# Window attention, forward and backward, on one core: y and z turned to token order by one DMA transpose per quad, the gradient turned on the PE array, and P and dS stacked into one stationary of 128 rows

## The chip, the core and the metric

One core of a Trainium2 chip runs the program. Its engines each work through their own list of instructions: PE (TensorE, the 128x128 matmul array; loads of its stationary operand are shown apart as PEld), DVE (VectorE), ACT (ScalarE), POOL (GpSimd) and SP (SyncE, which here only starts DMA transfers). Instructions of different engines wait for each other by semaphores. Matmuls write into PSUM, which has eight banks of 128 x 512 f32; DVE or ACT must move a result out (evict it) before its bank can be used again. The metric is the device time of one execution in microseconds; smaller is better.

## What is computed

Window attention over an image of 256 x 256 pixels with 384 channels in windows of 8 x 8 = 64 tokens, and its gradients with respect to x, wqkv and wo for a given grad_out:

```python
def _fwd_reference(x, wqkv, wo):
    ...
    xw = xw.reshape(B * nh * nw, win * win, C)
    qkv = xw @ wqkv
    q, k, v = (qkv[..., :C].copy(), qkv[..., C:2 * C].copy(), qkv[..., 2 * C:].copy())
    scale = C ** (-0.5)
    p = _softmax(jnp.einsum('bqc,bkc->bqk', q, k) * scale, axis=-1)
    o = jnp.einsum('bqk,bkc->bqc', p, v) @ wo
    ...
def reference(x, wqkv, wo, grad_out):
    _out, _vjp = jax.vjp(_f, x, wqkv, wo)
    _grads = _vjp(grad_out)
    return (_out0, *[jnp.asarray(_g) for _g in _grads])
```

All inputs and outputs are bf16. There are 1024 windows.

## The kernel before

The kernel never forms q, k and v. It folds the weights once at the start into four 384 x 384 matrices: A (query times key weights, scaled), its transpose AT, B (value times output weights) and its transpose BT. Per window, with x its tokens and g the incoming gradient, it computes y = x A and z = g BT (the program has them with channels on the partitions), the scores S = y x^T and the gradient of P, z x^T, in one PSUM tile `sd`, then P (softmax) and dS (`Sb`), u = x B, v = x AT, the output `po` = P u, and the gradient of x, `pd` = P^T z + dS^T y + dS v. For the weight gradients it forms `pu` = dS x and `pw` = P^T g per window and sums x^T times these over all windows into `GF_acc`.

Tiling: two windows, one above the other, make a tile of 128 tokens (`dram_tile`); the lower 64 partitions (`LO`) hold one window, the upper 64 (`HI`) the other. Four tiles make a quad; there are 128 quads. With 384 channels a row, `CK` = 3 blocks of 128 channels.

The main loop runs one `step` per quad, as a pipeline over three quads: c (the quad before), b (this quad) and a (the next). The order of every engine's instructions is the order in which `step` writes them (`manual_schedule`). In a step PE does, in this order: `scores` of b (24 matmuls); u and v (`uv`) of b's tiles 0 and 1; `attend` of c's tiles 0 and 1; a filler; `uv` of tiles 2 and 3; `yz_tok`, 24 PE transposes that turn y and z of b to token order; `attend` of c's tiles 2 and 3; `turn`, 16 small transposes of P and dS; `project` of a, 18 matmuls for z and y; a filler. A filler is one piece of `gf_group`: 12 matmuls that sum over three finished quads into one bank, and one addition into `GF_acc` by DVE. `soft` (on DVE and ACT) is written between these pieces.

`attend` works on 64 x 64 blocks. Its inner function `both` issues four matmuls with 64 rows and 64 columns each, two windows times two results, which occupy the four quarters of the array; a tile has three such groups, of which three halves go to `pd`: `Pb` with `zq`, `Sb` with `yq`, `ST` with `vq`. The four results of a tile take four PSUM banks: ACT evicts `po` (to `osb`) and `pd` (to `dsb`), DVE evicts `pu` and `pw`.

PSUM: the pool `ring` has seven banks that all pieces share in the order in which they come free, and `ps_sd` has one for the scores. Before its first matmul, a piece waits for the eviction that gives back the bank it is to use.

Transfers: `load` reads four tiles of x on SP's queue and four of grad_out on POOL's, two quads ahead, and then has SP issue two DMA transposes of 12 blocks of 128 x 128 each, `dT` from the gradient and `xT` from x. The stores of `osb` go out on SP's queue, those of `dsb` on POOL's, in two halves per tile. SP and POOL also work strictly in order.

The tables that say which engine evicts what, and the pace of the pipeline, stand ahead of the loop:

```python
EV = {"z": "AAA", "y": "DAD", "u": "AAAA", "v": "AAAA", "o": "AAAA", "U": "DDDD", "W": "DDDD", "d": "AAAA"}
AHEAD = 2
```

Of the kernel before, what the change touches and what calls it, by code (L numbers as in the profile page):

```python
# [9 lines left out]
ALU = mybir.AluOpType  # L10
# [12 lines left out]
def kernel(  # L23
# [83 lines left out]
    def dram_tile(ap, bp, t):  # L107
        return ap[0, 2 * WIN * bp:2 * WIN * (bp + 1), WIN * t:WIN * (t + 1), :]

    LO, HI = slice(0, WT), slice(WT, P)  # L110

    def load(st):
        bp, t0 = st["at"]
        st["xq"] = xq = grp.tile([P, QUAD, C], BF16, tag="xq", name="xq", bufs=2 * GQ + 3)
        st["dq"] = dq = qp.tile([P, QUAD, C], BF16, tag="dq", name="dq", bufs=5)
        for t in range(QUAD):
            nc.sync.dma_start(out=xq[:, t, :], in_=dram_tile(x, bp, t0 + t))
            nc.gpsimd.dma_start(out=dq[:, t, :], in_=dram_tile(grad_out, bp, t0 + t))  # L118
        st["xT"] = xT = qp.tile([P, QUAD, CK, P], BF16, tag="xT", name="xT", bufs=3)
        st["dT"] = dT = qp.tile([P, QUAD, CK, P], BF16, tag="dT", name="dT")  # L120
        for src, dst in ((dq, dT), (xq, xT)):
            nc.sync.dma_start_transpose(out=dst[:].rearrange("p t m k -> p (t m) k"),
                                        in_=src[:].rearrange("p t c -> p (t c)"))

    ENG = {"D": nc.vector.tensor_copy, "A": nc.scalar.copy}

    def project(st, kind, mo):
        if kind == 0 and mo == 0:
            st["yz"] = qp.tile([P, CK, QUAD, 4, WT], BF16, tag="yz", name="yz")
            st["zc"] = qp.tile([P, CK, QUAD, 2, WT], BF16, tag="zc", name="zc")  # L130
        yz = st["yz"]
        wgt, src = ((BT_sb, st["dT"]), (A_sb, st["xT"]))[kind]
        pj = ring.tile([P, QUAD, 2, WT], F32, tag="r")
        for m in range(CK):
            nc.tensor.matmul(pj[:].rearrange("p t w k -> p (t w k)"), lhsT=wgt[:, m, mo * P:(mo + 1) * P],  # L135
                             rhs=src[:, :, m, :], start=(m == 0), stop=(m == CK - 1))
        if kind == 0:
            ENG[EV["z"][mo]](out=yz[:, mo, :, 0:4:3, :], in_=pj[:])  # L138
            nc.vector.tensor_copy(out=st["zc"][:, mo, :, :, :], in_=yz[:, mo, :, 0:4:3, :])
        else:  # L140
            ENG[EV["y"][mo]](out=yz[:, mo, :, 1:3, :], in_=pj[:])  # L141

    def scores(st):
        yz, xT = st["yz"], st["xT"]
        st["sd"] = sd = ps_sd.tile([P, QUAD, 2, WT], F32, tag="sd", name="sd")
        for t in range(QUAD):
            for w in range(2):
                for m in range(CK):
                    nc.tensor.matmul(sd[:, t, w, :],  # L149
                                     lhsT=yz[:, m, t, 2 * w:2 * w + 2, :].rearrange("p s k -> p (s k)"),  # L150
                                     rhs=xT[:, t, m, w * WT:(w + 1) * WT],
                                     start=(m == 0), stop=(m == CK - 1))
# [4 lines left out]
    def soft(st, step):  # L157
# [14 lines left out]
        elif step == 3:  # L172
# [4 lines left out]
            nc.vector.reciprocal(out=ri[:], in_=rs[:])  # L177
            st["Pb"] = Pb = qp.tile([P, QUAD, WT], BF16, tag="Pb", name="Pb")
            nc.vector.tensor_tensor(out=Pb[:], in0=ex[:], in1=over_k(ri[:]), op=ALU.mult)
        elif step == 4:  # L180
            st["pr"] = pr = sm.tile([P, QUAD, WT], F32, tag="pr", name="pr")
            for w, h in ((0, LO), (1, HI)):
# [3 lines left out]
        else:  # L186
            pd = sm.tile([P, QUAD, WT], F32, tag="pd")
            nc.vector.tensor_tensor(out=pd[:], in0=st["Pb"][:], in1=over_k(st["D"][:]), op=ALU.mult)
            st["Sb"] = Sb = qp.tile([P, QUAD, WT], BF16, tag="Sb", name="Sb")
            nc.vector.tensor_tensor(out=Sb[:], in0=st["pr"][:], in1=pd[:], op=ALU.subtract)  # L190

    def uv(st, t, part):
        if t == 0 and part == 0:
            for n in ("uq", "vq", "yq", "zq"):
# [8 lines left out]
    def yz_tok(st, t, part):  # L203
        src, dst = ((st["yz"][:, :, t, 1:3, :], st["yq"]), (st["zc"][:, :, t, :, :], st["zq"]))[part]
        pt = ring.tile([P, CK, P], BF16, tag="r")
        for m in range(CK):
            nc.tensor.transpose(pt[:, m, :], src[:, m, :, :].rearrange("p w k -> p (w k)"), ident[:])  # L207
        nc.vector.tensor_copy(out=dst[:, t, :].rearrange("p (m c) -> p m c", m=CK), in_=pt[:])

    def turn(st, kind):  # L210
        src, n = ((st["Pb"], "PT"), (st["Sb"], "ST"))[kind]
        st[n] = dst = qp.tile([P, QUAD, WT], BF16, tag=n, name=n)
        pt = ring.tile([P, QUAD, WT], BF16, tag="r")
        for t in range(QUAD):
            for h in (LO, HI):
                nc.tensor.transpose(pt[h, t, :], src[h, t, :], ident[h, h])  # L216
        nc.vector.tensor_copy(out=dst[:], in_=pt[:])

    def attend(st, t):
        bp, t0 = st["at"]  # L220
        if t == 0:
            st["Uq"] = grp.tile([P, QUAD, C], BF16, tag="Uq", name="Uq")
            st["Wq"] = grp.tile([P, QUAD, C], BF16, tag="Wq", name="Wq")
        po = ring.tile([P, C], F32, tag="r", name="po")
        pd = ring.tile([P, C], F32, tag="r", name="pd")
        pu = ring.tile([P, C], F32, tag="r", name="pu")
        pw = ring.tile([P, C], F32, tag="r", name="pw")

        def both(straight, crossed):
            for h, o, (dst, lhs, rhs, first, last) in ((LO, LO, straight), (LO, HI, crossed), (HI, LO, crossed),  # L230
                                                       (HI, HI, straight)):
                nc.tensor.matmul(dst[o, :], lhsT=st[lhs][h, t, :], rhs=st[rhs][h, t, :], start=first, stop=last)  # L232

        both((po, "PT", "uq", True, True), (pd, "Pb", "zq", True, False))
        osb = ob.tile([P, C], BF16, tag="o")
        ENG[EV["o"][t]](out=osb[:], in_=po[:])  # L236
        nc.sync.dma_start(out=dram_tile(out_0, bp, t0 + t), in_=osb[:])
        both((pu, "ST", "xq", True, True), (pd, "Sb", "yq", False, False))
        ENG[EV["U"][t]](out=st["Uq"][:, t, :], in_=pu[:])  # L239
        both((pw, "Pb", "dq", True, True), (pd, "ST", "vq", False, True))  # L240
        dsb = ob.tile([P, C], BF16, tag="d")
        ENG[EV["d"][t]](out=dsb[:], in_=pd[:])  # L242
        for h, w in ((LO, 1), (HI, 0)):
            nc.gpsimd.dma_start(out=dram_tile(out_1, bp, t0 + t)[WIN * w:WIN * (w + 1)], in_=dsb[h, :])  # L244
        ENG[EV["W"][t]](out=st["Wq"][:, t, :], in_=pw[:])  # L245

    fill = []

# [17 lines left out]
            except StopIteration:  # L266
                fill.pop(0)

    def step(c, b, a):

        def on(st):
            return (lambda f, *r: f(st, *r)) if st is not None else (lambda f, *r: None)
        C_, B, A = on(c), on(b), on(a)
# [8 lines left out]
        C_(attend, 0)  # L282
        B(soft, 3)
        C_(attend, 1)
        B(soft, 4)
        filler(1)
        B(uv, 2, 0)
        B(uv, 2, 1)
        B(soft, 5)
        B(uv, 3, 0)  # L290
        B(uv, 3, 1)
        for t in range(QUAD):
            B(yz_tok, t, 0)
            B(yz_tok, t, 1)
        C_(attend, 2)
        C_(attend, 3)
        B(turn, 0)
        B(turn, 1)
        for kind in range(2):
            for mo in range(CK):  # L300
                A(project, kind, mo)
        filler(1)

    EV = {"z": "AAA", "y": "DAD", "u": "AAAA", "v": "AAAA", "o": "AAAA", "U": "DDDD", "W": "DDDD", "d": "AAAA"}
# [3 lines left out]
    AHEAD = 2  # L308
    with tc.manual_schedule(engines=MANUAL):
        for i in range(min(AHEAD, n)):  # L310
            load(sts[i])
        held = []
        get = lambda i: sts[i] if 0 <= i < n else None
        for i in range(-1, n + 1):
            if AHEAD <= i + AHEAD < n:
                load(sts[i + AHEAD])
            step(get(i - 1), get(i), get(i + 1))
            if i > 0:
                held.append(sts[i - 1])
                sts[i - 1] = None  # L320
# [64 lines left out]
```

## Time and profile before

| | |
|---|---|
| median of three runs | 2295.58 us (2294.31 to 2297.17) |
| the profiled execution | 2295.61 us, its span 2293.8 us |
| PE busy | 2231.7 us (97% of the span), clock 1.00 |
| DVE, ACT, POOL busy | 1827.0, 1259.5, 867.2 us |
| transposes of y and z on PE (L207), 128x128 | 3072, of 219 ns each with its pipeline |
| their copies out of PSUM by DVE (L208) | 1024, 346 and 345 ns |
| matmuls of `attend` (L232), 64x64 with 384 columns | 6144, 325 to 341 ns with their pipeline |
| DMA transposes on SP's queue | 256, of 12 blocks |
| bytes moved by DMA | 308.59 MB |

The profile is that of one execution. The chain of work that ended last is followed back from the last instruction: at each step to what released it. A matmul's duration in a table is longer than the time it holds the array, since matmuls are pipelined; the time that the array is held is the distance from one start to the next. Releasers, in square brackets, are inferred from semaphores. `pj`, `pt`, `pg`, `po`, `pd`, `pu` and `pw` are PSUM tiles: projections and u, v (`pj`), transposes (`pt`), fillers (`pg`) and the four results of `attend`.

### The profile page before, as it was taken

The page shows a single profiled execution, that of the slowest core. Times are in us where ns is not written, and L with a number is a line of the kernel's source. Part 1 is how long each engine was busy: PE and PEld are TensorE (multiplying, and loading weights), DVE is VectorE, ACT ScalarE, POOL GpSimd, SP SyncE. Part 2 cuts the span into 40 slices and gives each one's busy share as a digit, 9 for nine tenths or more (in the row PEclk, how much of TensorE's full clock was granted, in tenths as well). Part 3 has the DMA queues.
Part 4 walks back from the last instruction along what each step waited for, and adds up shares of the span by engine and source line. Part 5 has one row for each costly group of instructions (what it writes and reads, how often), then busy time and mean ns, then how long its engine had stood idle before and what let it go on. Part 6 is the DMA issues. An engine that isn't in the chain of part 4 may idle for free.

```text
span 2293.8 us, 59316 instructions
## 1 busy us (share of the span) xinstructions
PE 2231.7 (97%) x22910; PEld 1334.9 (58%) x22910; DVE 1827.0 (80%) x4771; ACT 1259.5 (55%) x2701; POOL 867.2 (38%) x1542
## 2 busy tenths in 40 slices
PE   7999999999999999999999999999999999999998
PEld 4555555555555555555555555555555555555555
DVE  6878887888788878877887788778878887888786
ACT  4555555555555555555555555555555555555553
POOL 3443333334333343343334333433333343334332
PEclk9999999999999999999999999999999999999999
DMA  7666555665565556555656565656556655655542
GB/s 165 143 142 135 137 131 135 138 139 133 138 139 132 133 138 138 133 135 135 142 131 142 134 141 128 143 134 138 129 135 139 139 132 139 138 133 134 137 114 60
DMA packets 624475, 308.59 MB, mean 135 GB/s; under 512 B 458816, under 2 KB 607040, under 8 KB 624192
## 3 DMA queue, kind: packets, MB, share of 16 engines
q1 hardware_dynamic: 550064, 203.49, 42.1%
q0 software_dynamic: 73728, 101.02, 15.6%
q8 instruction: 179, 2.93, 0.5%
q14 instruction: 104, 0.85, 0.1%
q10 hardware_dynamic: 400, 0.29, 0.0%
HBM read 101.84 MB, written 101.84 MB: 89 GB/s over the span
## 4 chain that ended last, share of the span: by engine, by line
PE 95%; ACT 3%; DVE 1%; issue 0%; DMA 0%; ACTq 0%
PE pg L256 22%; PE pj L135 22%; PE pj L199 21%; PE pt L207 7%; PE po L232 5%; PE pw L232 5%; PE sd L149 4%; PE pd L232 3%; PE pu L232 2%; PE pt L216 2%; ACT osb L236 2%; PE pc L97 0%; ACT uq L201 0%; DMA w_sb<-in_wqkv_dram 0%; ACT vq L201 0%
## 5 line engine op out<-in xcount | busy, mean ns | idle before, releaser
L244 POOL DMA_DIRECT2D out_dram<-dsb x1024 | 575.9, 570 | 1388.2 <-ACT dsb L242 1365.6
L201 ACT CAST uq<-pj 128x384 bf16<-128x384 f32 x512 | 245.3, 479 | 635.1 <-PE pj L199 632.9
L256 PEld LDWEIGHTS <-xq 128*128 128x128 bf16 x3072 | 290.1, 98 | 217.3 <-issue 21.9
L199 PEld LDWEIGHTS <-xT 128*128 128x128 bf16 x3072 | 291.6, 98 | 182.3 <-issue 0.5
L239 DVE CAST Uq<-pu 128x384 bf16<-128x384 f32 x512 | 280.9, 549 | 80.2 <-PE pu L232 80.2
L236 ACT CAST osb<-po 128x384 bf16<-128x384 f32 x512 | 247.2, 483 | 163.0 <-PE po L232 146.2
L199 PE MATMUL pj<-B_sb,xT 128*128 128x384 bf16 x1536 | 333.5, 326 | 0.0
L199 PE MATMUL pj<-AT_sb,xT 128*128 128x384 bf16 x1536 | 333.3, 326 | 0.0
L118 POOL DMA_DIRECT2D dq<-in_grad_out_dram x512 | 291.8, 579 | 12.8 <-issue 11.4
L245 DVE CAST Wq<-pw 128x384 bf16<-128x384 f32 x512 | 279.4, 546 | 0.0
L138 ACT CAST yz<-pj 128x512 bf16<-128x512 f32 x384 | 225.1, 586 | 97.3 <-PE pj L135 81.6
L258 DVE TENSOR_TENSOR GF_acc<-pg,GF_acc 128x384 f32<-128x384 f32 x258 | 143.8, 557 | 167.7 <-PE pg L256 163.8
L256 PE MATMUL pg<-Uq,xq 128*128 128x384 bf16 x1536 | 271.2, 327 | 0.0
L135 PE MATMUL pj<-dT,BT_sb 128*128 128x512 bf16 x1152 | 270.8, 380 | 0.2
L256 PE MATMUL pg<-Wq,xq 128*128 128x384 bf16 x1536 | 270.5, 326 | 0.0
L135 PE MATMUL pj<-xT,A_sb 128*128 128x512 bf16 x1152 | 269.5, 379 | 0.0
L242 ACT CAST dsb<-pd 128x384 bf16<-128x384 f32 x512 | 251.9, 492 | 6.6 <-PE pw L232 0.3
L201 ACT CAST vq<-pj 128x384 bf16<-128x384 f32 x512 | 245.3, 479 | 4.3
L141 DVE CAST yz<-pj 128x512 bf16<-128x512 f32 x256 | 175.9, 687 | 55.4 <-PE pj L135 55.4
L232 PE MATMUL pw<-dq,Pb 64*64 64x384 bf16 x1024 | 179.7, 330 | 40.0 <-ACT osb L236 40.0
L232 PEld LDWEIGHTS <-ST 64*64 64x64 bf16 x2048 | 147.6, 104 | 113.0 <-issue 102.0
L232 PE MATMUL po<-uq,PT 64*64 64x384 bf16 x1024 | 203.5, 337 | 0.2
(72 smaller groups left out, 3487.6 us busy)
## 6 DMA issues: line engine op xcount, KB each, us to landing
xq<-in_x_dram SPq DMA_DIRECT2D x512, 96.0 KB, 3.1
dq<-in_grad_out_dram POOLq DMA_DIRECT2D x512, 96.0 KB, 2.8
out_dram<-osb SPq DMA_DIRECT2D x512, 96.0 KB, 2.7
out_dram<-dsb POOLq DMA_DIRECT2D x1024, 48.0 KB, 2.6
dT<-dq SPq DMA_TRANSPOSE x128, 4.0
xT<-xq SPq DMA_TRANSPOSE x128, 4.3
w_sb<-in_wqkv_dram SPq DMA_DIRECT2D x1, 864.0 KB, 5.7
out_dram<-dw_sb SPq DMA_DIRECT2D x1, 864.0 KB, 3.8
```

The source lines that it names most:

```text
L118: nc.gpsimd.dma_start(out=dq[:, t, :], in_=dram_tile(grad_out, bp, t0 + t))
L135: nc.tensor.matmul(pj[:].rearrange("p t w k -> p (t w k)"), lhsT=wgt[:, m, mo * P:(mo + 1) * P], rhs=src[:, :, m, :], start=(m == 0), stop ...
L138: ENG[EV["z"][mo]](out=yz[:, mo, :, 0:4:3, :], in_=pj[:])
L199: nc.tensor.matmul(pj[:], lhsT=st["xT"][:, t, m, :], rhs=wgt[:, m, :], start=(m == 0), stop=(m == CK - 1))
L201: cp(out=dst[:, t, :], in_=pj[:])
L232: nc.tensor.matmul(dst[o, :], lhsT=st[lhs][h, t, :], rhs=st[rhs][h, t, :], start=first, stop=last)
L236: ENG[EV["o"][t]](out=osb[:], in_=po[:])
L239: ENG[EV["U"][t]](out=st["Uq"][:, t, :], in_=pu[:])
L242: ENG[EV["d"][t]](out=dsb[:], in_=pd[:])
L244: nc.gpsimd.dma_start(out=dram_tile(out_1, bp, t0 + t)[WIN * w:WIN * (w + 1)], in_=dsb[h, :])
L245: ENG[EV["W"][t]](out=st["Wq"][:, t, :], in_=pw[:])
L256: nc.tensor.matmul(pw[:], lhsT=st["xq"][:, t, ma * P:(ma + 1) * P], rhs=st["UW"[f] + "q"][:, t, :], start=(i == 0), stop=(i == n - 1))
```

## The change

y and z no longer go through the PE array to token order. Once z and y of a quad are evicted into `yz`, which holds z, y, y, z of the two windows side by side, SP issues one DMA transpose of 24 blocks into `tok`. A block of `tok` has 128 partitions: z's 64 tokens over y's for the one window, y's over z's for the other. To match it, `ps` holds P and dS stacked in the same manner: two ACT copies put P there, and the subtraction that gives dS, now in two halves, writes straight to the other 64 partitions. `attend` then opens `pd` with two matmuls of 128 rows and 64 columns in place of four of 64 rows and 64 columns.

The gradient's DMA transpose is gone: `grad_turn` transposes each of the four tiles in three PE transposes through a PSUM bank, and DVE copies the result to `dT`. `zc`, a copy of z, is no longer made, and `y` is evicted by ACT alone. The scores' bank joins the ring, which has eight banks now.

`step` is written in a new order and spans four quads (x is the quad after a). PE's order: scores of b, all of u and v of b, z's projection of a, a filler, `attend` of c's tiles 2 and 3, the turns, y's projection of a, a filler, `grad_turn` of x, `attend` of b's tiles 0 and 1. x and grad_out are both loaded on SP's queue, three quads ahead; both outputs are stored on POOL's queue in halves.

On PE, at the place where the transposes meet an attend. Before, the last y/z transpose and the first group of tile 2 (`zc` a copy of z, `PT` P turned, `zq` and `uq` z and u in token order):

```order
L207 LDWEIGHTS zc
L207 MATMUL pt<-ident,zc 128x128
L232 LDWEIGHTS PT
L232 MATMUL po<-uq,PT 64x384
L232 LDWEIGHTS Pb
L232 MATMUL pd<-zq,Pb 64x384
```

Now, at the end of a step, the last gradient transpose, the opening of `pd` for tiles 0 and 1, and the first results of tile 0:

```order
L135 LDWEIGHTS dq
L135 MATMUL pt<-ident,dq 128x128
L244 LDWEIGHTS ps
L244 MATMUL pd<-tok,ps 64x384
L244 LDWEIGHTS ps
L244 MATMUL pd<-tok,ps 64x384
L244 LDWEIGHTS ps
L244 MATMUL pd<-tok,ps 64x384
L244 LDWEIGHTS ps
L244 MATMUL pd<-tok,ps 64x384
L251 LDWEIGHTS ST
L251 MATMUL pu<-xq,ST 64x384
```

The transposes ahead of the attend are those of `dq`, and four matmuls with `ps`, two for each tile, stand ahead of the groups of four.

On DVE, the second half of a step. Before, from the last copies of y and z to the next softmax's maximum:

```order
L208 COPY yq<-pt 128x384
L208 COPY zq<-pt 128x384
L239 CAST Uq<-pu 128x384
L245 CAST Wq<-pw 128x384
L239 CAST Uq<-pu 128x384
L245 CAST Wq<-pw 128x384
L217 COPY PT<-pt 128x256
L217 COPY ST<-pt 128x256
L139 COPY zc<-yz 128x512 x3
L141 CAST yz<-pj 128x4x128 x2
L258 TENSOR_TENSOR GF_acc<-pg,GF_acc 128x384
L162 TENSOR_REDUCE mx<-sd 64x4 x2
```

Now, from the evictions of tile 2 to the same place:

```order
L260 CAST Uq<-pu 128x384
L267 CAST Wq<-pw 128x384
L260 CAST Uq<-pu 128x384
L267 CAST Wq<-pw 128x384
L233 COPY PT<-pt 128x256
L233 COPY ST<-pt 128x256
L280 TENSOR_TENSOR GF_acc<-pg,GF_acc 128x384
L136 COPY dT<-pt 128x384 x4
L260 CAST Uq<-pu 128x384
L267 CAST Wq<-pw 128x384
L260 CAST Uq<-pu 128x384
L267 CAST Wq<-pw 128x384
```

Eight copies per step (`yq`, `zq`), those of `zc` and two evictions of y are gone; four copies to `dT` stand behind the filler's addition and ahead of the evictions of tiles 0 and 1, which the next step's maximum follows directly.

On SP, one step's transfers. Before:

```order
L117 DMA xq<-in_x_dram 128x1x384 x4
L122 DMA_TRANSPOSE dT<-dq 128x12x128
L122 DMA_TRANSPOSE xT<-xq 128x12x128
L237 DMA out_dram<-osb 16x8x384 x4
L117 DMA xq<-in_x_dram 128x1x384 x4
```

Now:

```order
L118 DMA dq<-in_grad_out_dram 128x1x384
L117 DMA xq<-in_x_dram 128x1x384
L118 DMA dq<-in_grad_out_dram 128x1x384
L127 DMA_TRANSPOSE xT<-xq 128x12x128
L156 DMA_TRANSPOSE tok<-yz 128x24x128
L117 DMA xq<-in_x_dram 128x1x384
```

The stores have left SP's queue, the loads of the gradient have come to it (eight loads in turn, of which three are shown ahead), and the second transpose has 24 blocks and stands behind the step's own evictions of y.

The diff, cut where only names move:

```diff
-    ps_sd = ctx.enter_context(tc.tile_pool(name="ps_sd", bufs=1, space=bass.MemoryType.PSUM))
-    ring = ctx.enter_context(tc.tile_pool(name="ring", bufs=7, space=bass.MemoryType.PSUM))
+    ring = ctx.enter_context(tc.tile_pool(name="ring", bufs=8, space=bass.MemoryType.PSUM))
...
+    def grad_turn(st, t):
+        if t >= G_ON_PE:
+            return
+        pt = ring.tile([P, CK, P], BF16, tag="r")
+        for m in range(CK):
+            nc.tensor.transpose(pt[:, m, :], st["dq"][:, t, m * P:(m + 1) * P], ident[:])
+        nc.vector.tensor_copy(out=st["dT"][:, t, :, :], in_=pt[:])
...
+    def to_tokens(st):
+        st["tok"] = tok = qp.tile([P, CK, QUAD, 2, P], BF16, tag="tok", name="tok")
+        nc.sync.dma_start_transpose(out=tok[:].rearrange("p m t b k -> p (m t b) k"),
+                                    in_=st["yz"][:].rearrange("p m t s k -> p (m t s k)"))
...
+            st["ps"] = ps = qp.tile([P, 2, QUAD, WT], BF16, tag="ps", name="ps")
+            for w, h in ((0, LO), (1, HI)):
+                nc.scalar.copy(out=ps[h, w, :, :], in_=Pb[h, :, :])
...
-            st["Sb"] = Sb = qp.tile([P, QUAD, WT], BF16, tag="Sb", name="Sb")
-            nc.vector.tensor_tensor(out=Sb[:], in0=st["pr"][:], in1=pd[:], op=ALU.subtract)
+            ps = st["ps"]
+            for w, h, o in ((0, LO, HI), (1, HI, LO)):
+                nc.vector.tensor_tensor(out=ps[o, w, :, :], in0=st["pr"][h, :, :], in1=pd[h, :, :], op=ALU.subtract)
...
+        for t in pair:
+            pd = ring.tile([P, C], F32, tag="r", name="pd")
+            for w, o in ((0, HI), (1, LO)):
+                nc.tensor.matmul(pd[o, :], lhsT=st["ps"][:, w, t, :], rhs=st["tok"][:, :, t, w, :], start=True,
+                                 stop=False)
...
+            both(t, (pu, "ST", "xq", True), (po, "PT", "uq", True))
...
+            both(t, (pw, "Pb", "dq", True), (pd, "ST", "vq", False))
...
+            for dst, src in ((out_0, osb), (out_1, dsb)):
+                for h, w in ((LO, 1), (HI, 0)):
+                    nc.gpsimd.dma_start(out=dram_tile(dst, bp, t0 + t)[WIN * w:WIN * (w + 1)], in_=src[h, :])
...
+        B(uv, 2, 0)
+        B(uv, 2, 1)
+        B(uv, 3, 0)
+        B(uv, 3, 1)
+        B(soft, 4)
+        for mo in range(CK):
+            A(project, 0, mo)
+        B(soft, 5)
+        filler(1)
+        C_(attend, (2, 3))
+        B(turn, 0)
+        B(turn, 1)
+        for mo in range(CK):
+            A(project, 1, mo)
+        A(to_tokens)
+        filler(1)
+        for t in range(QUAD):
+            X(grad_turn, t)
+        B(attend, (0, 1))
...
+    G_ON_PE = QUAD
+    EV = {"z": "AAA", "y": "AAA", "u": "AAAA", "v": "AAAA", "o": "AAAA", "U": "DDDD", "W": "DDDD", "d": "AAAA"}
...
+    AHEAD = 3
```

More of the change, by code (lines that the diff above doesn't have):

```diff
@@ L201, in uv @@
         cp(out=dst[:, t, :], in_=pj[:])
[L203 to L208, printed above, removed]
     def turn(st, kind):
-        src, n = ((st["Pb"], "PT"), (st["Sb"], "ST"))[kind]
+        n = ("PT", "ST")[kind]
         st[n] = dst = qp.tile([P, QUAD, WT], BF16, tag=n, name=n)
@@ L214, in turn, with attend @@
         for t in range(QUAD):
-            for h in (LO, HI):
-                nc.tensor.transpose(pt[h, t, :], src[h, t, :], ident[h, h])
+            for w, o, h in ((0, LO, HI), (1, HI, LO)):
+                if kind == 0:
+                    nc.tensor.transpose(pt[o, t, :], st["Pb"][o, t, :], ident[o, o])
+                else:
+                    nc.tensor.transpose(pt[o, t, :], st["ps"][h, w, t, :], ident[h, h])
         nc.vector.tensor_copy(out=dst[:], in_=pt[:])
-    def attend(st, t):
+    def attend(st, pair):
@@ L220, in attend @@
         bp, t0 = st["at"]
-        if t == 0:
+        if pair[0] == 0:
             st["Uq"] = grp.tile([P, QUAD, C], BF16, tag="Uq", name="Uq")
             st["Wq"] = grp.tile([P, QUAD, C], BF16, tag="Wq", name="Wq")
[L224 to L242, printed above, removed]
@@ new lines, in both @@
+        def both(t, straight, crossed):
+            for h, o, (dst, lhs, rhs, first) in ((LO, LO, straight), (LO, HI, crossed), (HI, LO, crossed),
+                                                 (HI, HI, straight)):
+                nc.tensor.matmul(dst[o, :], lhsT=st[lhs][h, t, :], rhs=st[rhs][h, t, :], start=first, stop=True)
+        for t, pd in zip(pair, pds):
+            po = ring.tile([P, C], F32, tag="r", name="po")
+            pu = ring.tile([P, C], F32, tag="r", name="pu")
+            pw = ring.tile([P, C], F32, tag="r", name="pw")
+            both(t, (pu, "ST", "xq", True), (po, "PT", "uq", True))
+            osb = ob.tile([P, C], BF16, tag="o")
+            ENG[EV["o"][t]](out=osb[:], in_=po[:])
+            ENG[EV["U"][t]](out=st["Uq"][:, t, :], in_=pu[:])
+            both(t, (pw, "Pb", "dq", True), (pd, "ST", "vq", False))
+            dsb = ob.tile([P, C], BF16, tag="d")
+            ENG[EV["d"][t]](out=dsb[:], in_=pd[:])
+            for dst, src in ((out_0, osb), (out_1, dsb)):
+                for h, w in ((LO, 1), (HI, 0)):
+                    nc.gpsimd.dma_start(out=dram_tile(dst, bp, t0 + t)[WIN * w:WIN * (w + 1)], in_=src[h, :])
+            ENG[EV["W"][t]](out=st["Wq"][:, t, :], in_=pw[:])
@@ L307 @@
     n = len(sts)
-    AHEAD = 2
+    AHEAD = 3
     with tc.manual_schedule(engines=MANUAL):
```

52 lines of the change are left out of this document (22 added, 30 removed).

## The prediction

> **What bounds the kernel now.** I read the shares of busy time first, then the chain of work that ended last, by engine and by line.
>
> ```profile
> PE 2231.7 (97%) x22910; PEld 1334.9 (58%) x22910; DVE 1827.0 (80%) x4771; ACT 1259.5 (55%) x2701; POOL 867.2 (38%) x1542
> PE 95%; ACT 3%; DVE 1%; issue 0%; DMA 0%; ACTq 0%
> ```
>
> PE is busy for 97% of the span and carries 95% of the chain, so time is won only where PE issues less or waits less. PE's busy time hides waits, though, because the modelled end of a matmul reaches past the start of the next. I therefore took one whole step (one quad in each stage) from the chain in order of time, from the first u group to the end of the next scores; the columns are start, length, what.
>
> ```profile
> 999.66 1.95 PE pj L199 x12
> ...
> 1003.22 2.06 PE pg L256 x12
> 1005.27 1.95 PE pj L199 x12
> 1007.22 1.34 PE pt L207 x24
> 1008.56 0.28 PE po L232
> ...
> 1010.19 0.42 PE pt L216 x16
> 1010.61 3.99 PE pj L135 x18
> 1014.60 1.95 PE pg L256 x12
> 1016.55 0.70 PE sd L149 x24
> ```
>
> A step is 1016.55 + 0.70 - 999.66 = 17.59 us: u and v 3.90, attend of tiles 0 and 1 1.61 (999.66 + 1.95 = 1001.61 to 1003.22), two filler groups 4.01, the 24 y/z transposes 1.34, attend of tiles 2 and 3 1.63 (1008.56 to 1010.19), the turns 0.42, projections 3.99, scores 0.70. To see how much of the attends is waiting I read the timeline (start, length, engine, line, what).
>
> ```profile
> 1000.96 0.65 PE L199 MATMUL pj<-AT_sb,xT 128*128 128x384 bf16 x3
> ...
> 1001.54 0.35 PE L232 MATMUL po<-uq,PT 64*64 64x384 bf16 x1
> ...
> 1001.73 0.32 PE L232 MATMUL pu<-xq,ST 64*64 64x384 bf16 x1
> ...
> 1001.89 0.32 PE L232 MATMUL pw<-dq,Pb 64*64 64x384 bf16 x1
> ...
> 1002.86 0.32 PE L232 MATMUL pw<-dq,Pb 64*64 64x384 bf16 x1 [0.32 <-ACT osb L236]
> ...
> 1008.38 0.34 DVE L208 COPY zq<-pt 128x384 bf16<-128x384 bf16 x1
> ...
> 1008.64 0.35 DVE L208 COPY yq<-pt 128x384 bf16<-128x384 bf16 x1
> 1008.77 0.32 PE L232 MATMUL pu<-xq,ST 64*64 64x384 bf16 x1
> ...
> 1009.04 0.32 PE L232 MATMUL pw<-dq,Pb 64*64 64x384 bf16 x1
> ```
>
> Undisturbed, one group of four 64x64 matmuls lasts 0.16 us (1001.73 to 1001.89, the same as 384 columns on the full array). A pair of tiles has six groups: 0.98 us. The rest of 1.61 is one wait of about 0.5 us, in which the sixth group, pw, due at 1001.73 + 4 x 0.16 = 1002.37 but started at 1002.86, needs a PSUM bank that osb's eviction still holds, and a switch of the array's tile size: the 128x128 stream ends at 1000.96 + 3 x 0.163 = 1001.45 and the first 64x64 starts at 1001.54 (0.09). The switch back lies in the filler that follows: 2.06 us against 1.95 for the other filler (0.11). In the second pair the groups are 0.27 us apart (1008.77, 1009.04), which is the pace of DVE's copies (1008.38, 1008.64, 0.26 apart): each copy gives back the one bank that the next group needs. So of the 3.24 us of attending, 3.24 - 2 x 0.98 = 1.28 are waits for banks and switches.
>
> **The change on PE.** Removed: 24 transposes, 1.34 us, at 1.34 / 24 = 0.056 each. Added: 12 transposes of the gradient, 0.67. The gain is 0.67.
>
> The stacked stationary takes four of the 64x64 matmuls of a tile into two with 128 rows and 64 columns. Twelve matmuls in three groups become ten, in two groups of four and one of two. A group of four uses the whole array for 384 columns, and so would the two; I price the pair at the same 0.16. **So this edit alone wins nothing on PE**; it matches what the one DMA transpose delivers. No row shows two 128x64 matmuls beside each other. The nearest row, four matmuls in 0.16 of which two share their rows and differ in columns, says 0.16 for the pair; the other end, one after the other, is 0.33, or 4 x 0.163 = 0.65 us more per step. I take the nearer row and keep the other end. A gain is excluded, since both stream 384 columns.
>
> The Trainium skill, TensorEngine Tiling (Array Packing), section Available Configurations, lists 128x64 with two tiles, which speaks for 0.16; no run here shows it. The same page, Key Properties, says that a change of the tiling mode, not just of the tile, drains the array; the gaps of 0.09 and 0.11 above agree with that. By that rule the new size between 128x128 and 64x64 costs a further gap in each pair; without it the sum below would be 0.2 us per step lower.
>
> Switches go from four to six a step, at 0.10 from the two gaps. No row shows a switch to or from 128x64: I take the same 0.10, between 0 and twice that, so the two added ones are worth 0 to 0.4 us a step around the 0.2 that the sum holds.
>
> **The two attends after.** What paces them is the order in which the eight banks come back, and two latencies from the rows below: eviction starts 0.21 us after a matmul stream ends (1014.43 + 12 x 0.163 = 16.38, add at 16.59); osb's eviction lasts 0.47.
>
> ```profile
> 1002.02 0.42 ACT L171 ACTIVATE ex<-sh 128x256 f32<-128x256 f32 x1
> 1002.34 0.47 ACT L236 CAST osb<-po 128x384 bf16<-128x384 f32 x1
> ...
> 1014.43 2.11 PE L256 MATMUL pg<-Wq,xq 128*128 128x384 bf16 x12
> 1016.59 0.56 DVE L258 TENSOR_TENSOR GF_acc<-pg,GF_acc 128x384 f32<-128x384 f32 x1 [1.26 <-PE pg L256]
> ```
>
> Tiles 2 and 3, with 0 at the end of the filler ahead of them: switch 0.10, two pd pairs to 0.42, switch 0.10, pu and po to 0.67, pw to 0.84, pu and po to 1.00, pw to 1.16. The first turn takes the bank of the first osb: po's end 0.67 + 0.21 + 0.47 + 0.04 = 1.39 to 1.42. So **1.42**, of which 0.26 is that wait.
>
> Tiles 0 and 1, with 0 again at the end of the filler: transposes to 0.67; DVE adds the filler's group first (0.21 to 0.77), then the four gradient copies, at the pace of the yq and zq copies above (0.35 long, 0.26 apart), at 0.68, 0.94, 1.21, 1.47, with the bank back 0.39 after each start. Switch, pd pairs, switch to 1.18, pu and po to 1.34, pw (bank of copy 1, 1.07) to 1.50, the second po needs copy 3 (1.60) and ends at 1.77, the last pw copy 4 (1.86) and ends at 2.03; switch, scores at 2.13. That is 2.13 - 0.67 = **1.46**, with some 0.2 of bank waits left. The scores' bank comes from the first osb, 1.34 + 0.21 + 0.47 = 2.02: just in time.
>
> Sum: scores 0.70, u and v 3.90, projections 3.99, fillers 2 x 1.95 = 3.90 (the switch in 2.06 is counted in the attends), gradient transposes 0.67, turns 0.42, attends 1.42 + 1.46: **16.46 us**, 1.13 less. Over 128 steps that is 145 us. The profiled execution took 2295.61 us with a span of 2293.8, and the median is 2295.58, so no correction: **2150 us**. The 42 us outside 128 steps stay.
>
> **What is costed at nothing, and its cover.**
>
> ```profile
> 1003.71 0.42 DVE L179 TENSOR_TENSOR Pb<-ex,ri 128x256 bf16<-128x256 f32 x1
> ```
> ```profile
> 999.66:1017.25 17.59, 17.27 (x180) 10.34 (x179) 14.14 (x37) 9.79 (x21) 6.78 (x12) 1.00 0.58 137
> ```
> ```profile
> L138 ACT CAST yz<-pj 128x512 bf16<-128x512 f32 x384 | 225.1, 586 | 97.3 <-PE pj L135 81.6
> ```
> ```profile
> q1 hardware_dynamic: 550064, 203.49, 42.1%
> q0 software_dynamic: 73728, 101.02, 15.6%
> ```
> ```profile
> xT<-xq SPq DMA_TRANSPOSE x128, 4.3
> ```
>
> These are a row of the timeline, the step in the view by stretches (us, then the busy time of PE, PEld, DVE, ACT and POOL, the clock, the DMA share and GB/s), a group of the page, its two large DMA queues (packets, MB, share of 16 engines), and the time from issue to landing of a transpose.
>
> ACT has 9.79 us of work in the step. It gets two more y evictions (2 x 0.586) and two copies of P (256 elements a partition; the exponential of that width takes 0.42): 11.8 of 16.5. DVE loses eight copies, the zc copies and two y evictions and gets four copies and one more subtraction, so it falls below its 14.14. Both hide behind PE.
>
> The copies of P add a wait: ACT stands still until DVE has P, and the four last u and v evictions and three of z are queued behind it. P came 1003.71 + 0.42 - 999.66 = 4.5 us after the scores' end, where the softmax begins. In the changed order DVE still has four evictions of the attend ahead of it and begins about 1.5 us after the scores' start, so ACT is free again at 1.5 + 4.5 + 0.8 = 6.8. PE first needs one of those banks for tile 2's pd, 0.70 + 3.90 + 1.95 + 1.95 = 8.5 us in. Cover: 1.7 us; every us beyond it would cost 128 us.
>
> POOL issues 16 stores in place of 8 stores and 4 loads; at 6.78 / 12 = 0.57 each that is 9.1 us a step, below 16.5, and a store has half a step before its buffer is needed again.
>
> SP takes the gradient's loads and the y/z transpose, 24 blocks, in place of the gradient's 12. That transpose goes out when y is evicted and is read at the end of the next step, about 18 us later; a transpose of 12 blocks landed 4.3 us after issue, so at most 8.6 are expected. On the 16 engines: plain transfers of equal size are 101 MB on q0 for 15.6%, so of q1's 42.1% the transposes are 26.5%, 608 us / 256 = 2.4 us each. The step had 0.58 x 17.59 = 10.2 us of that work and gets 2.4 more: 12.6 of 16.46.
>
> **Rivals.**
> 1. *The bank waits go entirely* (DVE and ACT return banks sooner than I worked out): both pairs fall to 0.98 plus switches, 0.26 and 0.18 less: 16.02 us a step, 2094 us. For it: it needs only 0.2 to 0.3 us of earlier evictions. Against it: the paces are those of the same engines in the same situation.
> 2. *The 128x64 pairs run one after the other*: +0.65 us, 17.11: 2233 us. For it: never seen here. Against it: the 64x64 groups use columns side by side.
> 3. *The transposes become the bound, slower than before*: each 12 blocks take what the trace shows from issue to landing and nothing beside them: 3 x 4.3 = 12.9, and the plain work 31.2% of 17.9 = 5.6 behind: 18.5 us a step, 0.9 more than now, 2295 + 128 x 0.9 = 2410 us. It decides once the twelve added blocks cost over 17.59 - 10.2 = 7.4 us in place of 2.4. Against it: issue-to-landing holds fixed latency, and nothing on PE waits for a transfer now; for it, DMA would be 77% occupied.
> 4. *The change does not do what it says*: the waits move to where P's copies hold ACT and eat 1.1 us (the cover of 1.7 is gone and 1.1 more): about 2290 us.
>
> **How the numbers follow.** Forecast 2150 (2110 to 2190): 0.60. Rival 1, with cheaper switches down to about 2040: 0.14. Rival 2 and mixtures with other small waits, 2190 to 2270: 0.16. Rival 3: 0.06. Rival 4: 0.04, half of it within 0.2%, half faster by more. A measurement of this kernel tells 0.2% from no change. Faster by over 0.2% is 0.60 + 0.14 + 0.16 + 0.02 = 0.92, same 0.02, slower 0.06. The range reaches over the forecast, most of rival 1 and rival 2's point: 2070 to 2240.
>
> **What would show it.** In the changed profile: a step of about 16.5 us in the chain; 24 transposes gone and 12 of dq at 0.056 each; two pd matmuls of 128x64 starting within 0.02 us of each other (rival 2: 0.16 apart); a gap near 0.1 ahead of pd and again behind it; attend pairs of 1.4 and 1.5 us, with pw ending its waits on DVE's dT copies; no wait of PE for tok or xT (rival 3 would name the transfer). The prediction is wrong if ACT shows PE waiting for uq or vq evictions, if tok lands later than 18 us after issue, or if scores wait for osb by more than 0.1 us a step.

## The result and the profile after

The changed kernel takes 2152.74 us (median of four runs, 2151.99 to 2153.63) against 2295.94 before, a ratio of 0.9377 with a 95% interval of 0.9361 to 0.9393. The forecast was 2150 in a range of 2070 to 2240.

The page of the changed kernel, first the busy shares, then the chain by engine:

```profile
PE 2112.1 (98%) x20350; PEld 1204.6 (56%) x20350; DVE 1504.5 (70%) x3747; ACT 1444.5 (67%) x3213; POOL 1138.0 (53%) x2054
...
PE 82%; ACT 11%; issue 4%; DMA 2%; DVE 0%; POOL 0%; SPq 0%; ACTq 0%; POOLq 0%
```

PE still carries most of the chain, with ACT now in it. The same view of the chain in order of time, for one step (start, length, what):

```profile
1001.62 3.90 PE pj L219 x24
1005.52 1.94 PE pj L147 x9
1007.47 0.69 PE pg L278 x5
1008.15 1.48 ACT yz L150 x3
1009.63 0.60 issue
1010.24 0.49 ACT osb L259
...
1015.20 0.67 PE pt L135 x12
1015.87 0.45 PE pd L244 x4
...
1017.26 0.82 PE sd L165 x24
1018.08 3.90 PE pj L219 x24
```

From one u group to the next it is 1018.08 - 1001.62 = 16.46 us; the forecast's sum was 16.46. (The terms of that sum did not all come out; the errors cancelled, as shown further down.) The 24 transposes of 1.34 us are gone and 12 of 0.67 have come. The chain leaves PE in the filler and follows ACT's three z evictions to the first output eviction: the 0.60 of "issue" between them says that ACT was idle there, so that piece of the chain is no proof that ACT bounds; `p_copies_twice` below asks.

The timeline shows the two attends (start, length, engine, line, what):

```profile
1007.30 2.11 PE L278 MATMUL pg<-Wq,xq 128*128 128x384 bf16 x12
...
1009.35 0.52 PE L244 MATMUL pd<-tok,ps 128*64 128x384 bf16 x4
...
1009.79 0.35 PE L251 MATMUL pu<-xq,ST 64*64 64x384 bf16 x1
...
1010.77 0.25 PE L230 MATMUL pt<-ident,Pb 64*64 64x64 bf16 x5
...
1010.84 0.22 PE L232 MATMUL pt<-ident,ps 64*64 64x64 bf16 x2
...
1011.15 2.10 PE L147 MATMUL pj<-xT,A_sb 128*128 128x512 bf16 x9
...
1015.04 0.83 PE L135 MATMUL pt<-ident,dq 128*128 128x128 bf16 x12
...
1015.71 1.14 DVE L136 COPY dT<-pt 128x384 bf16<-128x384 bf16 x4
...
1017.22 0.86 PE L165 MATMUL sd<-xT,yz 128*128 128x64 bf16 x24
```

The four 128x64 matmuls fill 1009.35 to 1009.79: two pairs of 0.163 and a switch of 0.11, so the two of a pair run beside each other. Tiles 2 and 3 take from the filler's stream end, 1007.30 + 12 x 0.163 = 1009.26, to the first turn at 1010.77: 1.51. Tiles 0 and 1 take from 1015.04 + 0.67 = 1015.71 to the scores at 1017.22: also 1.51.

The DMA queues of the page, and the landing of the transposes:

```profile
q1 hardware_dynamic: 746672, 253.82, 59.3%
q0 software_dynamic: 98304, 101.32, 17.6%
```
```profile
xT<-xq SPq DMA_TRANSPOSE x128, 4.0
tok<-yz SPq DMA_TRANSPOSE x128, 7.7
```

Together 77% of the engines' time, as worked out, and no row of the waits names PE waiting for `tok` or `xT`.

### The profile page after: what moved, and what is told of

Its sections match the earlier page's. It is cut to its first block, busy times and chain, and to the rows that moved or that the text cites. A ratio compares the mean times of both kernels' runs of the same rounds, so it can differ in the third digit from the quotient of the medians.

```text
span 2150.8 us, 54406 instructions
## 1 busy us (share of the span) xinstructions
PE 2112.1 (98%) x20350; PEld 1204.6 (56%) x20350; DVE 1504.5 (70%) x3747; ACT 1444.5 (67%) x3213; POOL 1138.0 (53%) x2054
## 4 chain that ended last, share of the span: by engine, by line
PE 82%; ACT 11%; issue 4%; DMA 2%; DVE 0%; POOL 0%; SPq 0%; ACTq 0%; POOLq 0%
PE pj L147 23%; PE pj L219 22%; PE pg L278 16%; ACT yz L150 8%; PE sd L165 5%; PE pt L135 4%; PE pd L244 3%; ACT osb L259 3%; PE pu L251 3%; PE pw L251 2%; PE pt L230 1%; DMA out_dram<-dsb 1%; PE pt L232 1%; PE po L251 1%; POOL out_dram L266 0%
## 5 line engine op out<-in xcount | busy, mean ns | idle before, releaser
L266 POOL DMA_DIRECT2D out_dram<-osb x1024 | 572.2, 563 | 951.7 <-ACT osb L259 928.0
L278 PEld LDWEIGHTS <-xq 128*128 128x128 bf16 x3072 | 300.1, 98 | 226.3 <-DVE pr L202 2.2
L263 ACT CAST dsb<-pd 128x384 bf16<-128x384 f32 x512 | 254.4, 497 | 15.0 <-DMA out_dram<-dsb 14.4
L221 ACT CAST vq<-pj 128x384 bf16<-128x384 f32 x512 | 250.2, 489 | 2.0
L152 ACT CAST yz<-pj 128x512 bf16<-128x512 f32 x384 | 225.1, 586 | 31.6
L150 ACT CAST yz<-pj 128x512 bf16<-128x512 f32 x384 | 206.0, 640 | 1.8 <-PE pj L147 1.7
L198 ACT COPY ps<-Pb 64x256 bf16<-64x256 bf16 x256 | 103.2, 403 | 149.7 <-DVE Pb L195 148.2
L251 PE MATMUL pu<-xq,ST 64*64 64x384 bf16 x1024 | 185.1, 338 | 0.4
L147 PEld LDWEIGHTS <-BT_sb 128*128 128x128 bf16 x1152 | 112.7, 98 | 123.0 <-issue 0.9
```

The source lines that it names most:

```text
L266: nc.gpsimd.dma_start(out=dram_tile(dst, bp, t0 + t)[WIN * w:WIN * (w + 1)], in_=src[h, :])
L278: nc.tensor.matmul(pw[:], lhsT=st["xq"][:, t, ma * P:(ma + 1) * P], rhs=st["UW"[f] + "q"][:, t, :], start=(i == 0), stop=(i == n - 1))
```

## Experiments

All are edits of the changed kernel (2152.7 us), some of them on top of another. Each was timed in three rounds (the last in five) against the kernel before, which took 2295.5 to 2296.0 in these comparisons.

### Where the 143 us come from: transposes or order

`yz_pe` keeps everything else that is new (order, eight banks, stacked stationary, queues, evictions) and puts the transposes back on the engines where they were: y and z on PE, now behind y's projection, and the gradient by DMA.

```diff
+            nc.tensor.transpose(pt[:, m, :], st["yz"][:, m, t, 2 * b:2 * b + 2, :].rearrange("p s k -> p (s k)"), ident[:])
+        nc.vector.tensor_copy(out=st["tok"][:, :, t, b, :], in_=pt[:])
...
-        A(to_tokens)
+        for t in range(QUAD):
+            B(tok_on_pe, t, 0)
+            B(tok_on_pe, t, 1)
...
-    G_ON_PE = QUAD
+    G_ON_PE = 0
```

> The new order, eight shared banks and the stacked stationary stay, but the token-order tiles are made by 24 PE transposes and 8 DVE copies a step, ahead of the second filler, and the gradient is turned by DMA as before the change: the transposes stand where they stood before, all else is new. Theory 1 (PE's sum): 16.46 - 0.67 - 0.09 + 1.34 = 17.04 us a step, about 2227 us, so that 69 us of the gain came from order and banks and 74 from the transposes. Rival (the moved transposes are the whole gain, the order is worth nothing): about 2296. Rival (the order is the whole gain): about 2153.

Measured: 2237.46 us, ratio 0.9744 (0.9729 to 0.9758). Both rivals fall. Of 143 us, 58 came with all the rest that is new (2296 to 2237.5) and 85 with the moved transposes (2237.5 to 2152.7); the forecast had 0.67 x 128 = 86 for the transposes and 59 for the rest. The miss against 2227 is 10 us, 0.08 a step: the expectation had booked 0.09 for an attend of tiles 0 and 1 that no longer waits for copies, but in this trace it takes 1.42 us from its first matmul to the scores, the same as in the changed kernel (1015.80 to 1017.22). `grad_early` below shows why. Where the 58 lie can be read from the starts of the matmuls (median over the steps of each trace): the two attends, with the switch ahead of them, take 3.31 us a step before the change and 3.03 here, and the turns of P and dS 0.53 and 0.38. No run separates the order from the stacking.

`banks7` gives the scores their own bank again and leaves seven to the ring.

```diff
+    ps_sd = ctx.enter_context(tc.tile_pool(name="ps_sd", bufs=1, space=bass.MemoryType.PSUM))
+    ring = ctx.enter_context(tc.tile_pool(name="ring", bufs=7, space=bass.MemoryType.PSUM))
...
+        st["sd"] = sd = ps_sd.tile([P, QUAD, 2, WT], F32, tag="sd", name="sd")
```

> The changed kernel with seven shared banks and a bank of the scores' own, as before the change. Theory (an attend of two tiles takes eight banks in a row): the eighth must then wait for the first osb eviction of its own attend: 0.15 us more in tiles 2 and 3, 0.22 more in tiles 0 and 1: 0.37 us a step, about 2200. Rival (the eighth bank is worth nothing, order and transposes are all): 2153.

Measured: 2225.56 us, ratio 0.9693 (0.9677 to 0.971): 73 us, more than the 47 expected. Its chain in tiles 2 and 3:

```profile
1012.74 0.49 ACT osb L260
1013.23 0.04 issue
1013.27 0.32 PE pw L252
```

The last pw starts when the first osb eviction of the same attend has ended, as the theory says. So the eighth bank in the ring is worth 0.57 us a step here. That is 0.2 more than worked out, and most of it can be found in the trace: tiles 2 and 3 take 0.16 longer (0.15 expected), tiles 0 and 1 0.29 (0.22 expected), and the turns, for which nothing had been booked, 0.46 (1013.43 to 1013.89) in place of 0.38. The 73 us cannot be subtracted from the 58, since no run has both seven banks and the transposes where they were; what the order alone brings stays open.

### What holds the attends: copies, osb, or the filler's bank

`grad_early` moves the gradient's transposes ahead of the second filler.

```diff
         A(to_tokens)
+        for t in range(QUAD):
+            X(grad_turn, t)
         filler(1)
-        for t in range(QUAD):
-            X(grad_turn, t)
         B(attend, (0, 1))
```

> grad_turn stands ahead of the second filler, so DVE's four copies run beside the filler and no bank of the attend of tiles 0 and 1 waits for them. Theory (bank waits by the order in which banks come back): that attend falls from 1.51 to 1.28, but then the scores wait for the first osb eviction until 1.42, so 0.09 us a step, 12 us: about 2141. If DVE's pace were the whole 0.23: 2123. If the waits are not DVE's: 2153.

Measured: 2153.51 us, ratio 0.9382 (0.9368 to 0.9396), no change, by the number the case in which the waits are not DVE's. The chain shows what is there instead:

```profile
1017.36 0.45 PE pd L244 x4
1017.80 0.28 PE pu L251
...
1018.18 0.49 ACT osb L259
1018.67 0.04 issue
1018.71 0.86 PE sd L165 x24
```

The copies are out of the chain, and the scores now wait for the first osb eviction until the very moment at which they started anyway. The two waits lay side by side and ended together; the 1.42 that I had worked out for the second was 0.09 too early.

`pd_last` puts the 128x64 matmuls behind the groups of four, so that evictions start sooner; `pd_last_grad_early` does both.

```diff
-        for t, pd in zip(pair, pds):
+        for t in pair:
...
+            both(t, (pu, "ST", "xq", True), (po, "PT", "uq", True))
...
+            both(t, (pw, "Pb", "dq", True), (pd, "ST", "vq", False))
...
+        for t, (pd, osb) in zip(pair, pds):
+            for w, o in ((0, HI), (1, LO)):
+                nc.tensor.matmul(pd[o, :], lhsT=st["ps"][:, w, t, :], rhs=st["tok"][:, :, t, w, :], start=False,
+                                 stop=True)
```

> In both attends the four 128x64 matmuls into pd come last instead of first, so that the first output eviction starts 0.43 us sooner; the number of matmuls and of switches stays. Theory (banks): tiles 2 and 3 fall from 1.51 to 1.27 us (no wait of the turn for osb), but tiles 0 and 1 now need the banks of DVE's four gradient copies one after the other ahead of pd and grow from 1.51 to 1.88: 16.59 us a step, about 2170, slower than the change itself. Rival (the attends are bound by matmul time and switches, not banks): 2153, no change. Rival (only the wait for osb counts, not the copies): 2092 to 2122.

> Both: the copies are out of the way and the evictions start sooner. Theory (banks): both attends at 1.27 us, all matmuls and three switches and nothing else, 0.48 us a step less: 15.98, about 2091. If the two edits only added up: 2141 + 2170 - 2153, about 2158.

Measured: `pd_last` 2175.5 us, ratio 0.9481 (0.9465 to 0.9496), slower than the change by 23 where 17 were expected; `pd_last_grad_early` 2153.03, ratio 0.9377 (0.9363 to 0.9391), where 2091 were expected. A miss of 62 us, and the timeline of the latter says why:

```profile
1019.41 0.35 PE L243 MATMUL pu<-xq,ST 64*64 64x384 bf16 x1
...
1019.51 0.56 DVE L279 TENSOR_TENSOR GF_acc<-pg,GF_acc 128x384 f32<-128x384 f32 x1 [1.30 <-PE pg L277]
...
1019.92 0.32 PE L243 MATMUL pw<-dq,Pb 64*64 64x384 bf16 x1
...
1020.13 0.35 PE L243 MATMUL pd<-vq,ST 64*64 64x384 bf16 x2
...
1020.41 0.52 PE L260 MATMUL pd<-tok,ps 128*64 128x384 bf16 x4
...
1020.86 0.87 PE L165 MATMUL sd<-xT,yz 128*128 128x64 bf16 x24
```

In this order the eighth bank is wanted with the second tile's pw at 1019.92, 0.51 us after the attend's first matmul, and it is the filler's: DVE's addition returns it at 1019.51 + 0.56 = 1020.07, and pd starts at 1020.13, 0.21 behind its pw, with which it would start if its bank were free. I had booked that bank as free in time. Three waits of about the same length, for the copies, for osb and for the filler's addition, thus lie beside each other; taking away one or two of them shows the third. That the filler's bank is the third is read from this trace; no run takes it away.

### How much cover ACT's copies of P have

```diff
+            for _ in range(2):
-            for w, h in ((0, LO), (1, HI)):
-                nc.scalar.copy(out=ps[h, w, :, :], in_=Pb[h, :, :])
+                for w, h in ((0, LO), (1, HI)):
+                    nc.scalar.copy(out=ps[h, w, :, :], in_=Pb[h, :, :])
```

> ACT makes its two copies of P twice, 0.82 us more ahead of the last four u and v evictions and the three of z; nothing else changes. Prediction's cover (1.7 us until PE needs a bank that is queued behind the copies): 2153, no change. Reading of the timeline after (z's last eviction ends 0.61 ahead of the first output eviction, and the second po needs z's last bank 0.5 later): about 0.2 us a step are lost, 2179. Reading of the chain after (it runs through ACT's z evictions, so ACT bounds the step there): nearly all of 0.82 is lost, about 2250.

Measured: 2177.41 us, ratio 0.9484 (0.947 to 0.9499): 24.7 us for 105 us of added work. So 0.82 - 24.7 / 128 = 0.63 us a step are covered, neither 1.7 nor none. Of the three readings on record before the run, the one from the timeline, 2179, came out. The timeline of ACT, and what PE does next in the chain:

```profile
1003.42 1.69 ACT L199 COPY ps<-Pb 64x256 bf16<-64x256 bf16 x4 [1.16 <-DVE Pb L195]
...
1006.62 1.61 ACT L150 CAST yz<-pj 128x512 bf16<-128x512 f32 x3
1008.05 0.56 ACT L260 CAST osb<-po 128x384 bf16<-128x384 f32 x1
```
```profile
1008.28 0.35 PE po L252 x2
```

z's evictions now run straight into osb's; in the changed kernel 0.60 us of idle time lay between them. The second po of the attend now starts 0.05 after z's last eviction has ended (1006.62 + 1.61 = 1008.23), whose bank it needs. That gap, within 0.03 us, was the cover.

### The gradient back on DMA

`grad_half` and `grad_dma` set the constant that says how many of a quad's four gradient tiles go over PE, the first to two, the second to none.

```diff
-    G_ON_PE = QUAD
+    G_ON_PE = 2
```
```diff
-    G_ON_PE = QUAD
+    G_ON_PE = 0
```

> Two of the four gradient tiles go by DMA (6 blocks more, 42 a step), two by PE. Theory 1 (PE's sum): 6 transposes less, 0.33 us, and about 0.09 of bank waits: 16.04 us a step, about 2099 us. Theory 2 (DMA fills up): the load would be 12.9 + 1.2 = 14.1 of 16.0 us, 88%, so a part of the 54 us is lost again, and what is lost shows as waits for transfers.

> The gradient goes back to a DMA transpose of 12 blocks, so SP transposes 48 blocks a step and PE none of the gradient. Theory 1 (the step is the sum of PE's pieces): 12 transposes less, 0.67 us, and the attend of tiles 0 and 1 no longer waits for DVE's gradient copies, 0.09 more (then the first output eviction sets the scores): 16.46 - 0.76 = 15.70 us a step, about 2056 us. Theory 2 (48 blocks fill the DMA engines: 77% of 16.8 us now, 12.9, plus 2.4 is 15.3 of 15.7): transfers land late and PE waits for them, 2090 us or more, with PE's waits naming dT, xT or tok, or output buffers waiting for their stores. If the reorder alone had won and the transposes on PE had cost nothing: 2153, no change.

Measured: `grad_half` 2121.3 us, ratio 0.9241 (0.9226 to 0.9257); `grad_dma` 2142.92, ratio 0.9327 (0.9308 to 0.9347). These lie 22 and 87 us above PE's sum. Some 11 us of each are the 0.09 x 128 that the expectations had booked for the gradient copies and that `grad_early` showed to be worth nothing. In `grad_dma` PE's weight loads waited for `dT` 79 times, 86.7 us in all, and the timeline of SP's queue is full:

```profile
1004.56 2.20 SPq L127 DMA_TRANSPOSE dT<-dq  x1
1006.81 2.42 SPq L127 DMA_TRANSPOSE xT<-xq  x1
1009.33 6.23 SPq L156 DMA_TRANSPOSE tok<-yz  x1
1015.60 0.59 SPq L117 DMA_DIRECT2D xq<-in_x_dram  x1
```

Eight loads of 0.6 (one took 1.06), then 2.2, 2.4 and 6.2, with 0.1 or less between them, are the whole step. That leaves two readings: SP's time to issue, or DMA engines (98% by the page) that hold SP up. `grad_dma_pool` moves the four loads of the gradient from SP to POOL:

```diff
-            nc.sync.dma_start(out=dq[:, t, :], in_=dram_tile(grad_out, bp, t0 + t))
+            nc.gpsimd.dma_start(out=dq[:, t, :], in_=dram_tile(grad_out, bp, t0 + t))
```

> As grad_dma (the gradient transposed by DMA, 48 blocks a step), but the four gradient loads of a step are issued by POOL again, which frees SP of 4 x 0.65 = 2.6 of the 16 us that it was busy. Theory A (in grad_dma SP's time to issue was the bound): the step falls to about 16.3 - 2.6 or PE's 15.8, whichever is longer: 2060 to 2080, POOL at 16 stores and 4 loads x 0.57 = 11.4 us has room. Theory B (the 16 DMA engines are the bound, 98% occupied): 2143 within 0.5%, and the issue of tok's transpose stays stretched.

Measured: 2080.51 us, ratio 0.9065 (0.9051 to 0.9078), 62 us less than `grad_dma` with the same bytes. The page of this faster run:

```profile
q1 hardware_dynamic: 873648, 253.80, 72.8%
q0 software_dynamic: 122880, 151.68, 30.6%
```

The shares add up to 103%, so the share counts packets that wait beside each other and isn't the part of a capacity that is used up. SP's queue shows the rest:

```profile
1008.34 2.93 SPq L127 DMA_TRANSPOSE xT<-xq  x1
1014.43 3.98 SPq L156 DMA_TRANSPOSE tok<-yz  x1
```

Between these two SP now stands idle for 3.2 us, and `tok` takes 4.4 in place of 5.6 (medians of the two traces), where the rival expected it to stay as long. SP's time to issue was the bound. Why the same transpose holds SP longer in one run than in another (`xT` 1.7 in the changed kernel, 2.7 here) is not shown. The Trainium skill, Trainium Kernel Development and Optimization, section Key Constraints, says that issuing from several engines only saves the sequencer's issue time; that agrees with this pair of runs, and here that time was the 62 us.

`half_ob4` asks whether `grad_half` loses time on output buffers, and adds a fourth of each kind.

```diff
-    ob = ctx.enter_context(tc.tile_pool(name="ob", bufs=3))
+    ob = ctx.enter_context(tc.tile_pool(name="ob", bufs=4))
```

> As grad_half, with four output buffers of each kind instead of three. In grad_half the step of the chain was 16.12 us, 2109 by PE's sum, and 2121 was measured; ACT waited 12.1 + 16.6 us in all for output buffers whose stores had not landed. If that is where the 12 us went: 2109 to 2114. If not: 2121.

Measured: 2113.62 us, ratio 0.9207 (0.9193 to 0.9221), at the upper end of what was expected if the buffers were the cause. They are 8 of the 22 us; with the 11 above, some 3 stay open. `pd_last_early_half` sets G_ON_PE = 2 in `pd_last_grad_early`:

> The same with two of the four gradient tiles transposed by DMA. PE's sum: 0.33 us less, 15.65 us a step, 2049. DMA: grad_half lost some 12 us of its 43 already, and 14.1 us of DMA work in 15.65 is 90%, so 2055 to 2080, with output buffers or transposes named in the waits.

Measured: 2119.56 us, ratio 0.9232 (0.9219 to 0.9246), the time of `grad_half`; its expectation rested on the 2091 that had already failed.

### Transposes on DMA, loads on POOL and a fourth buffer

`grad_dma_pool_ob4` takes `grad_dma_pool` and the fourth buffer: no gradient transposes on PE, x's loads on SP, the gradient's on POOL.

> grad_dma_pool with four output buffers of each kind. Its chain shows a step of 15.79 us, which is 2067 by the sum, and 2080.5 was measured; ACT waited 66.3 + 20.1 us for buffers whose stores had not landed (3.9 us to landing, 2.9 in the changed kernel). In half_ob4 the fourth buffer recovered 7.7 us. If the stores' landing is what is left: 2067 to 2073. If it is the order of POOL's queue (loads ahead of stores): 2080.

Measured: 2064.72 us, ratio 0.8992 (0.898 to 0.9004), 88 us below the change itself and 16 below `grad_dma_pool`. The stores' landing was what was left, and the order of POOL's queue falls as a rival.

## Why the prediction was right, point by point

**PE is the bound and its sum is the step.** The bound is right, and the sum came out to 0.01 us a step. That it came out so closely is luck: the attends were 0.14 too short in it and the turns with the projections 0.15 too long. `yz_pe` confirms the split: 85 us for the moved transposes (86 forecast), 58 for the rest (59).

**The stacked stationary wins nothing on PE.** The timeline agrees: two pairs in 0.33 us, the same as two groups of four. The rival with 0.16 more per tile falls. The switches, taken at 0.10, are 0.09 ahead of pd (1009.26 to 1009.35) and 0.11 behind it. To open pd with 64x64 matmuls on the stacked tiles was not tried.

**The attends.** Forecast 1.42 and 1.46, measured 1.51 each, 0.14 too short together. The order of events was right. In tiles 0 and 1 the second po and the last pw, forecast at 1.60 and 1.86 behind the filler for DVE's third and fourth copy, start in the trace at 1016.64 and 1016.90, 1.60 and 1.86 behind 1015.04. The term that was mis-sized is the way to the first osb: I took 0.21 us from stream end to eviction, the filler's, where po's took 0.28 (1009.79 + 0.163 to 1010.24). So the scores' bank, forecast as just in time, became the last wait of tiles 0 and 1, and the turn of tiles 2 and 3 came later. Rival 1, that the waits go away, did not come about, and three experiments show how firmly they hold: each took away one or two of them and none gained.

**The turns.** Turns and projections were put at 4.41 us and took 0.38 (1010.77 to 1011.15) and 2 x 1.94, 4.26. This hid the miss in the attends. The 0.42 for the turns had been taken over from the old step as if it were work alone. Before the change the two groups of eight stood 0.28 apart and the turns took 0.53:

```profile
1009.70 0.54 DVE L239 CAST Uq<-pu 128x384 bf16<-128x384 f32 x1
...
1010.01 0.31 PE L216 MATMUL pt<-ident,Pb 64*64 64x64 bf16 x8
...
1010.29 0.31 PE L216 MATMUL pt<-ident,Sb 64*64 64x64 bf16 x8
...
1010.54 2.12 PE L135 MATMUL pj<-dT,BT_sb 128*128 128x512 bf16 x9
```

The first eight start within 0.12 us of each other in the trace; the second eight begin 0.05 after DVE has evicted `Uq` (1009.70 + 0.54 = 1010.24), so they waited for that bank. In the changed kernel the second group starts 0.07 behind the first (1010.77, 1010.84), with the first still running. In `pd_last_grad_early` the two start 0.03 apart:

```profile
1014.47 0.22 PE L230 MATMUL pt<-ident,Pb 64*64 64x64 bf16 x2
...
1014.50 0.22 PE L232 MATMUL pt<-ident,ps 64*64 64x64 bf16 x2
...
1014.74 2.12 PE L147 MATMUL pj<-xT,A_sb 128*128 128x512 bf16 x9
```

There the projection follows 0.27 after the first transpose. So the turns are a piece in which bank waits were hidden, and their 0.15 a step, 19 us, belongs to the 58. By the code the two groups now lie in different quarters of the array; whether they could run beside each other in the same ones is not shown.

**ACT's cover.** The forecast named 1.7 us, up to the bank of tile 2's pd. Two steps of it failed. ACT is through with the copies earlier than the 6.8 us after the scores' start that were worked out:

```profile
1005.69 0.82 ACT L198 COPY ps<-Pb 64x256 bf16<-64x256 bf16 x2 [1.16 <-DVE Pb L195]
```

They end at 1006.51, and these scores start one step ahead of 1017.22, at 1000.76: 5.75 us. But the bank that counts is another: behind the copies ACT also holds z's evictions and then the first osb, and there the cover is 0.63. It cost nothing, because 0.63 is enough.

**DMA.** The share (77%) and the landing of `tok` (7.7 us, at most 8.6 forecast) were right, and nothing on PE waits for it. That a store has time to land before its buffer is needed again held less well: ACT waited 14.4 us in all for stores of `dsb`, a term that was put at nothing. A fourth buffer was tried in `half_ob4` and `grad_dma_pool_ob4`, not in the changed kernel itself. Rival 3 was built on the wrong resource: what fills up with more transposes is SP's time to issue (loads 8 x 0.6, `xT` 1.7, `tok` 4.2 of 16.46 in the changed kernel, all of the step in `grad_dma`), not the engines' share.

## What to carry to other kernels

Where an engine is busy for 97%, take one step of its chain apart, count the matmul streams by starts, and call the rest waits; look for waits inside the small pieces too. The sum came out to 0.01 us here because errors of 0.14 and 0.15 cancelled. The waits for PSUM banks came in bundles that end together: removing one was worth only the distance to the next, so look for the next before booking the gain. Before moving work to DMA, add up the issuing queue's own time; a share of 100% on the engines did not bound, a full queue did.

## What the runs showed that was not expected

A DMA transpose occupies SP for long: 4.2 us for 24 blocks and 1.7 for 12 in the changed kernel, against 0.6 for a 96 KB load, and 6.2 for the 24 in the step of `grad_dma` shown above. One more PSUM bank in the shared ring was worth 73 us. Two groups of eight small transposes ran beside each other as soon as both had a bank: the 16 took 0.38 us in the changed kernel and 0.27 in `pd_last_grad_early`, against 0.53 before the change, with a wait for a bank in between.
